# Last stage of an attention and two-MLP kernel: the out-projection as seven products of halves, and x read back as prepared parts

## The chip, the cores and the metric

The kernel runs on one core of a Trainium2 chip. A core has TensorE (PE in the profile; its weight loads are shown apart as PEld), VectorE (DVE), ScalarE (ACT), GpSimd (POOL) and SyncE (SP), whose queue issues all of this kernel's DMA transfers, in its program order. The metric is device time in microseconds (us); lower is better.

## The reference

Inputs are fp32. Block-causal attention is followed by two MLPs; each MLP's activations stand between its two matrices.

```python
def _moe_ref(x, w_in, w_out):      # x [2304, 512], w_in [512, 2048], w_out [2048, 512]
    h = x @ w_in
    g = h * np.cos(h)
    return (g @ w_out).astype(np.float32)
...
    r = np.maximum(h, 0.0)         # second MLP: same shapes, own weights
    g = r * r
    return (g @ w_out).astype(np.float32)
...
    attn_out = _attn_ref(**attn_kwargs)      # 4 batches, 8 heads, 576 rows, 64 wide
    x = np.ascontiguousarray(attn_out.transpose(0, 2, 1, 3)).reshape(B * S, H * D)
    x = _moe_ref(x=x, **moe_kwargs)
    return _moe2_ref(x=x, **moe2_kwargs)
```

## The kernel before

**Precision.** Every large product is taken in parts: an operand is split into a rounded part ("hi", an fp32r tile, made by `hi_part`) and the rest ("lo", by `lo_part`), and `mm3` issues three matmuls: hi*hi, hi*lo, lo*hi. A split costs one ScalarE and one VectorE instruction as a rule.

**Stages.** The 2048 wide middle of each MLP is cut in four column groups of 512. Attention runs first, together with the first half of MLP 1's middle (`first_in`, `first_out`, results kept in DRAM as `y1_d`). Then a loop over `stage` does the rest: stage 0 is the second half of MLP 1 and adds `y1_d`, giving `y_d`; stage 1 is the first half of MLP 2, kept in DRAM as `y2_d`; stage 2, the last, is the second half of MLP 2 and adds `y2_d`, giving `out`. Each stage goes over five chunks of tokens: four of 512 and one of 256 (called chunk 4).

**In-projection.** In these stages h is computed by seven products of halves instead of eight (`quad`, Winograd's form of Strassen's method): x and the weight block are each cut into 2 x 2 quarters, seven sums or differences of quarters ("forms") are split into hi and lo, and seven products of 256 x 256 by 256 tokens, 12 matmuls each, are accumulated in three PSUM banks `a`, `b`, `c`. `load_quarters` loads a chunk of x, makes the four sums and the seven splits, in every stage anew. Chunk 4 goes without (`two`, `load_plain`). The weights' forms are made once by `left_parts` ("staging") and kept in DRAM as `wi_d`; `factors` loads them.

**Out-projection.** In stages 1 and 2, for each 128 tokens, 24 matmuls with g as the stationary operand and 512 columns of `w2_out` as the moving one are accumulated in one PSUM bank `y`; VectorE adds `y2` in stage 2, and a DMA writes 128 tokens. The weights come as raw words of 8 bytes, are converted and split by `weights` (eight pieces per stage).

**Order.** Nothing is issued as the code is written: `Recorder` records operations and a list scheduler (`schedule`) puts them in order, with tables of numbers (`BIAS`, `PUT_OFF`, `LATE` and the like). The order on each engine is fixed when the program is built; an instruction that waits holds up all that stand behind it on its engine or queue.

Of the kernel before, what the change touches and what calls it, by code (L numbers as in the profile page):

```python
# [24 lines left out]
BIAS = [{"DVE": 1.89, "ACT": 0.46, "POOL": 0.26}, {"DVE": 2.58, "ACT": -0.56, "POOL": 0.68}, {"DVE": -0.3, "ACT": -2.99, "POOL": 0.29}, {"DVE": -1.17, "ACT": -3.72, "POOL": 2.36}]  # L25
# [14 lines left out]
PUT_OFF = [{"load": 114, "weights": -25, "prep": 11, "scores": 21, "weighted": -156, "split": 287, "in": 62, "cos": -140, "out": -54, "warm": 9160, "later": 877}, {"load": 381, "weights": -104, "prep": -71, "scores": 69, "weighted": -789, "split": 92, "in": 43, "cos": -127, "out": -24, "later": 911}, {"load": 543, "weights": 771, "prep": 52, "scores": 520, "weighted": 66, "split": 1698, "in": 0, "cos": -391, "out": -77, "later": 696}, {"in": 92, "out": 124, "later": -317}]  # L40
# [99 lines left out]
class Recorder:  # L140
# [9 lines left out]
    LATE, SLACK, EXTRA = 2497, 4, 16  # L150
# [204 lines left out]
def f(v):  # L355
    return v.bitcast(F32)
# [7 lines left out]
def kernel(  # L364
# [251 lines left out]
    y2_d = T(dram, [NT // 128, 128, DM], F32, "y2_d")  # L616
    wi_d = [[T(dram, [128, 2, 512], F32, f"wi_d{c}{i}") for i in range(7)] for c in range(6)]
# [134 lines left out]

    @of("weights")
    def left_parts(w, k, to):
# [3 lines left out]
        s1, s2, s3, s4 = [T(st_p, [128, 256], F32, f"ws{i}") for i in range(4)]  # L758
# [4 lines left out]
        cs = slice(k * 256, k * 256 + 256)  # L763
        for t, x in zip(to, (a11, a12, s4, a22, s1, s2, s3)):
            st = T(st_p, [128, 2, 256], F32R, "so", 2)
            hi_part(st[:, 0], x)
            lo_part(st[:, 1], x, st[:, 0])
            dma(t[:, :, cs], f(st), 262144)

    @of("later")  # L770
    def left_weights(w, c, to):

        gate = R.ops[-1:]
        for k in range(2):
            left_parts([weight_piece(w[i * 128:i * 128 + 128, c * 512:c * 512 + 512], gate) for i in (k, k + 2)], k, to)

# [66 lines left out]
    def in_cos(tmp, w_in, xs, g, n):  # L843

        for m in range(HALF):
# [8 lines left out]
            hi_part(g[0][:, m, :n], r)  # L854
            lo_part(g[1][:, m, :n], r, g[0][:, m, :n])

    @of("out")
    def out_T(w_out, g, n, sink):

        for d in range(KD):  # L860
            ps = bank("y")[:, :n]
            for m in range(HALF):
# [3 lines left out]
                    ps, (hi[m % 4][:, c], lo[m % 4][:, c]), (g[0][:, m, :n], g[1][:, m, :n]), m == 0, m == HALF - 1  # L866
# [256 lines left out]
    xs = {}  # L1123
# [12 lines left out]
    def new_g():  # L1136
        return [T(g_p, [128, HALF, 512], F32R, f"g{i}") for i in "hl"]
# [276 lines left out]
```

## Time and profile before

| What | Value |
|---|---|
| Median of 3 runs | 1003.09 us (1002.53 to 1003.45) |
| The profiled execution's own time | 1003.07 us |
| Span of the profiled execution, first to last instruction | 1001.3 us |
| TensorE busy | 978.8 us, 98% |
| VectorE, ScalarE, GpSimd busy | 663.3, 636.6, 203.6 us |
| DMA moved | 150.10 MB, mean 150 GB/s |
| Stage 2 | from about 805 us of the span to its end |

A matmul's duration in the trace includes its way through the array, and matmuls overlap, so the distance between the starts of two matmuls is what one costs; the busy share alone does not say that the engine does useful work all the time. "Idle before" and "waited for" are times in which an engine had nothing to do, with the instruction that ended it.

### The profile page before, as it was taken

What the parts mean: (1) busy time and instruction counts of PE and PEld (TensorE: products, weight loads), DVE (VectorE), ACT (ScalarE), POOL (GpSimd) and SP (SyncE); (2) the same over time, 40 slices, a digit from 0 to 9 for tenths busy, and PEclk for the clock granted to TensorE, in tenths of its full rate; (3) what the DMA queues carried; (4) which work ended last, traced back from release to release, by engine and by line L of the source; (5) the groups of instructions that cost most, each with busy time, mean ns of one, the idle gap of its engine ahead of it and who ended that gap; (6) DMA issues with size and microseconds to landing.
All of it is one profiled execution on the core that took longest, in us unless ns stands there. A gap on an engine that the chain in (4) does not pass through costs nothing.

```text
span 1001.3 us, 18384 instructions
## 1 busy us (share of the span) xinstructions
PE 978.8 (98%) x6672; PEld 862.2 (86%) x6672; DVE 663.3 (66%) x1469; ACT 636.6 (64%) x1423; POOL 203.6 (20%) x281
## 2 busy tenths in 40 slices
PE   7879999999999999999999999999999999999998
PEld 5647987889888989999898989898988898988987
DVE  4668565667676756485877977956859395835523
ACT  7898688898998996473675865654556471413301
POOL 4666143274554541000033100000000000000000
PEclk8979999999999999999999999999999999999999
DMA  7644233356555448822535698325366843222111
GB/s 191 183 132 124 59 90 88 101 137 182 172 171 170 149 146 298 310 68 85 172 102 167 206 305 312 126 85 189 119 219 210 323 161 98 68 67 64 43 64 43
DMA packets 136506, 150.10 MB, mean 150 GB/s; under 512 B 70368, under 2 KB 102624, under 8 KB 136416
## 3 DMA queue, kind: packets, MB, share of 16 engines
q1 hardware_dynamic: 136416, 148.93, 47.5%
q8 instruction: 53, 0.87, 0.4%
q14 instruction: 37, 0.30, 0.1%
HBM read 99.09 MB, written 49.81 MB: 149 GB/s over the span
## 4 chain that ended last, share of the span: by engine, by line
PE 89%; DVE 4%; ACT 3%; POOL 2%; issue 1%; DMA 1%; SPq 0%; POOLq 0%; DVEq 0%
PE y L530 40%; PE h L530 35%; PE t L547 6%; PE a L540 4%; PE s L540 3%; PE s L530 1%; DVE c L431 1%; DVE s L431 1%; DVE r L424 1%; POOL e L513 1%; ACT e L415 1%; POOL c L717 1%; DVE gl L472 0%; DMA raw<-in_moe_w_in_dram 0%; ACT c L415 0%
## 5 line engine op out<-in xcount | busy, mean ns | idle before, releaser
L530 PE MATMUL h<-xh,w 128*128 128x256 f32 x1536 | 289.1, 283 | 0.1
L530 PEld LDWEIGHTS h<-xh,w 128*128 128x128 f32 x1536 | 244.3, 191 | 2.6 <-ACT p L483 0.4
L530 PE MATMUL y<-gh,w 128*128 128x256 f32 (+2 forms) x832 | 211.8, 330 | 6.2 <-POOL w L449 3.2
L530 PE MATMUL h<-xl,w 128*128 128x256 f32 x768 | 216.6, 283 | 0.0
L530 PE MATMUL y<-w,gh 128*128 128x512 f32 x576 | 185.1, 395 | 0.0
L530 PEld LDWEIGHTS y<-gh,w 128*128 128x128 f32 x832 | 143.3, 189 | 20.0 <-issue 4.6
L530 PEld LDWEIGHTS h<-xl,w 128*128 128x128 f32 x768 | 146.9, 191 | 1.1
L530 PE MATMUL y<-gl,w 128*128 128x256 f32 (+2 forms) x416 | 135.6, 329 | 0.8 <-DVE gl L472 0.8
L530 PEld LDWEIGHTS y<-w,gh 128*128 128x128 f32 x576 | 107.6, 188 | 25.0 <-DVE w L472 0.2
L530 PE MATMUL y<-w,gl 128*128 128x512 f32 x288 | 113.8, 395 | 0.0
L454 ACT ACTIVATE gh<-r 128x512 fp32r<-128x512 f32 (+2 forms) x138 | 76.6, 556 | 50.5 <-DVE r L1292 34.0
L472 DVE TENSOR_TENSOR gl<-r,gh 128x512 fp32r<-128x512 f32 (+2 forms) x135 | 85.7, 639 | 27.6 <-ACT gh L454 24.9
L957 DVE CUSTOM_DVE_ANT_0 e<-s,mask 128x384 f32<-128x384 f32 (+4 forms) x160 | 71.0, 478 | 30.4 <-PE s L540 22.1
L513 POOL TENSOR_SCALAR e<-e,st 128x256 f32<-128x256 f32 (+4 forms) x124 | 75.3, 621 | 75.3 <-DVE st L978 55.6
L415 ACT ACTIVATE e<-e,st 128x128 f32<-128x128 f32 (+4 forms) x144 | 82.8, 578 | 4.9 <-DVE st L957 2.7
L530 PEld LDWEIGHTS y<-gl,w 128*128 128x128 f32 x416 | 78.2, 189 | 6.9 <-DVE gl L472 1.3
L424 DVE TENSOR_TENSOR o<-y,y 128x512 f32<-128x512 f32 (+1 forms) x38 | 25.2, 662 | 83.0 <-PE y L530 80.3
L483 ACT ACTIVATE p<-h 128x512 f32<-128x512 f32 x48 | 28.5, 593 | 74.7 <-PE h L530 74.7
L547 PE MATMUL t<-ident,e 128*128 128x128 f32 (+1 forms) x400 | 65.6, 288 | 2.2 <-POOL e L513 2.1
L530 PEld LDWEIGHTS y<-w,gl 128*128 128x128 f32 x288 | 54.1, 188 | 12.7
L483 ACT ACTIVATE r<-t 128x384 f32<-128x384 f32 (+1 forms) x110 | 56.1, 533 | 12.8 <-PE t L547 11.9
L530 PE MATMUL h<-xs2h,w 128*128 128x320 f32 x256 | 61.5, 313 | 0.0
(139 smaller groups left out, 1758.5 us busy)
## 6 DMA issues: line engine op xcount, KB each, us to landing
wi_d<-so SPq DMA_DIRECT2D x84, 256.0 KB, 3.0
w<-wi_d SPq DMA_DIRECT2D x42, 512.0 KB, 6.4
raw<-in_moe_w_in_dram SPq DMA_DIRECT2D x32, 512.0 KB, 5.1
raw<-in_moe_w_out_dram SPq DMA_DIRECT2D x32, 512.0 KB, 4.2
y<-y_d SPq DMA_DIRECT2D x34, 256.0 KB, 2.9
y_d<-o SPq DMA_DIRECT2D x34, 256.0 KB, 2.8
x<-y_d SPq DMA_DIRECT2D x16, 512.0 KB, 4.0
k<-in_k_dram SPq DMA_DIRECT2D x36, 128.0 KB, 2.8
```

The source lines that it names most:

```text
L415: return nc.scalar.activation(real(out), real(in_), func, **kw)
L424: out.size / 0.96 + 68, lambda: nc.vector.tensor_tensor(real(out), real(a), real(b), op=op), [out], [a, b],
L431: lambda: nc.vector.scalar_tensor_tensor(real(out), real(a), s, real(b), op0=op0, op1=op1),
L454: "ACT": ("ACT", n / 1.2 + 92, lambda: nc.scalar.activation(real(hi), real(x), ACTF.Copy)),
L472: lambda: nc.vector.tensor_tensor(real(lo), real(x), real(f(hi)), op=ALU.subtract), 1,
L483: "ACT": ("ACT", n / 1.2 + 50, lambda: nc.scalar.activation(real(out), real(ps), ACTF.Copy)),
L513: lambda: nc.gpsimd.tensor_scalar(real(out), real(x), real(s), 1.0, op0=ALU.mult, op1=ALU.mult),
L530: lambda: nc.tensor.matmul(real(ps), lhsT=real(lhsT), rhs=real(rhs), start=start, stop=stop, skip_group_check=True),
L540: nc.tensor.matmul(real(ps), lhsT=real(l), rhs=real(r), start=start, stop=stop, skip_group_check=True)
L547: lambda: nc.tensor.transpose(real(out), real(in_), real(ident)[0:rows, 0:rows]), [out], [in_, ident],
L717: lambda: nc.gpsimd.tensor_tensor(real(wi), real(t), real(wi), op=ALU.subtract), 1,
L957: lambda: nc.vector.tensor_tensor_reduce(out=real(e), in0=real(ps), in1=real(m), scale=-1.0, scalar=BIG, op0=ALU.add, op1=ALU.min, accum_o ...
```

## The change

Stage 2's out-projection is done by seven products as well. For each of the two column groups of 512, g (squared h) is cut into 2 x 2 quarters of 256 x 256 tokens; `formed` makes the seven forms of g out of `quad`'s four results with four sums, and splits each. `w2_out`'s forms are made by `right_parts_of` in stages 0 and 1, kept in DRAM as `wf_d`, and loaded by `right_factors` into tiles that stage 2 has no other use for. `out_quad` multiplies: per chunk seven products, each of 24 matmuls with 256 columns (12 in chunk 4, whose four quarters have 128 tokens). `second` adds the partial results in PSUM to `y2`, seven adds per chunk. The 14 splits and 8 sums per chunk replace 8 splits.

Stage 1 now writes each split form of x to DRAM (`xp_d`, 24 transfers of 512 KB) for the four chunks that it takes first; stage 2 loads these instead of `y_d`, with no sums and no splits. Stage 1 takes the chunks in the order 0, 4, 1, 2, 3, and stage 2 in the order 3, 0, 1, 2, 4, so that chunk 3's forms are still in place when stage 2 begins. Output and `y2` transfers are 256 tokens by 256 columns. `g` becomes eight small tiles, the output tile has four buffers instead of two, and the scheduler's tables are other ones, so the order changes in every stage.

```diff
-BIAS = [{"DVE": 1.89, "ACT": 0.46, "POOL": 0.26}, {"DVE": 2.58, "ACT": -0.56, "POOL": 0.68}, {"DVE": -0.3, "ACT": -2.99, "POOL": 0.29}, {"DVE": -1.17, "ACT": -3.72, "POOL": 2.36}]
+BIAS = [{"DVE": 1.72, "ACT": 0.3, "POOL": 0.23}, {"DVE": 3.65, "ACT": -0.74, "POOL": -0.23}, {"DVE": 0.06, "ACT": -1.78, "POOL": 0.06}, {"DVE": -1.43, "ACT": -5.31, "POOL": 1.15}]
...
-    LATE, SLACK, EXTRA = 2497, 4, 16
+    LATE, SLACK, EXTRA = 1369, 0, 27
...
+    def right_parts_of(w, k, to):
+        b11, b12, b21, b22 = [x[:, o:o + 256] for x in w for o in (0, 256)]
+        t1, t2, t3, t4 = four_sums()
+        add(t1, b12, b11, ALU.subtract)
+        add(t2, b22, t1, ALU.subtract)
+        add(t3, b22, b12, ALU.subtract)
+        add(t4, b21, t2, ALU.subtract)
+        stage_parts((b11, b21, b22, t4, t1, t2, t3), k, to)
...
+            if keep is not None:
+                dma(keep[j], f(t).rearrange("p j k c -> p (j k c)"), 524288)
...
+    def kept_parts(keep, which):
+        ops = {}
+        for j in which:
+            t = x_tile(j)
+            dma(f(t).rearrange("p j k c -> p (j k c)"), keep[j], 524288)
+            ops[j] = t[:, 0], t[:, 1]
+        return ops
...
+            if (i, j) == (0, 1):
+                add(a22, a21, a22)
+                add(a21, a11, a21, ALU.subtract)
+                add(a11, a22, a11, ALU.subtract)
+                split(4, a22)
+                split(5, a11)
+                split(6, a21)
+            if len(parts) == 4:
+                add(a12, a12, a11, ALU.subtract)
+                split(2, a12)
...
+        def times_(ps, i, first):
+            for t in range(nt):
+                cs = slice(t * 128, t * 128 + 128)
+                for q in range(2):
+                    (gh, gl), (wh, wl) = g[q][i], w[q][i]
+                    for m in range(2):
+                        mm3(
+                            ps[:, t], (gh[:, m, cs], gl[:, m, cs]), (wh[:, m], wl[:, m]),
+                            first and not t + q + m, q + m == 2, (a, b, c),
+                        )
+
+        times_(a, 0, True)
+        finish(0, 0, a, False)
+        times_(b, 1, True)
+        finish(0, 0, b, True)
+        times_(a, 5, False)
+        finish(0, 1, a, False)
+        times_(c, 4, True)
+        finish(1, 1, c, False)
+        times_(a, 6, False)
+        finish(1, 1, a, True)
+        times_(c, 2, False)
+        finish(0, 1, c, True)
+        times_(a, 3, False)
+        finish(1, 0, a, True)
...
+        def finish(h, d, ps, last):
+            t, r0 = ys[h, d], c0 + h * nt * 128
+            tt(t, ps, t, ALU.add)
+            if last:
+                dma(out[r0:r0 + nt * 128, d * 256:d * 256 + 256].rearrange("(t p) d -> p t d", p=128), t, nt * 131072)
...
+    ROUNDS = (0, 1, 2, 3, 4), (0, 4, 1, 2, 3), (3, 0, 1, 2, 4)
...
+                if turn_:
+                    xs = kept_parts(xp_d[i], FIRST if i < 4 else (0, 1, 4))
+                g = g_forms()
...
+            if (stage, turn_) in ((0, 3), (1, 0)):
+                right_weights(w2_out, 2 + stage, wf_d[stage])
```

**Where it moves instructions.** First place: VectorE at the very end of the program, chunk 4 of stage 2. In the names `h` is an in-projection's PSUM bank, `s` and `r` are squared h, `y` an out-projection's bank, `o` an output tile, and the tiles `gh`, `gl` followed by a number are, after the change, places of forms of g (each holds a form's hi and lo). Before, the last two in-projection banks (`h_12077`, `h_12107`) and the out-projection's adds:

```order
L424 TENSOR_TENSOR s_12111<-h_12077,s_12111 128x512
L472 TENSOR_TENSOR gl_12071<-s_12111,gh_12063 128x2x256
L424 TENSOR_TENSOR s_12140<-h_12107,s_12140 128x512
L472 TENSOR_TENSOR gl_12071<-s_12140,gh_12063 128x2x256
L424 TENSOR_TENSOR o_12169<-y_12137,y2_11997 128x512
L424 TENSOR_TENSOR o_12195<-y_12167,y2_12054 128x512
```

After the change, from the last in-projection bank (`h_12625`) to the form that the out-projection's fourth product needs:

```order
L424 TENSOR_TENSOR s_12694<-h_12625,s_12694 128x512
L424 TENSOR_TENSOR o_12473<-y_12666,o_12473 128x256
L472 TENSOR_TENSOR gh2_12706<-s_12694,gh2_12706 128x2x128
L472 TENSOR_TENSOR gl2_12708<-s_12694,gl2_12708 128x2x128
L733 TENSOR_TENSOR s_12694<-s_12670,s_12694 128x2x128
L733 TENSOR_TENSOR s_12670<-s_12670 128x2x128
L424 TENSOR_TENSOR o_12473<-y_12667,o_12473 128x256
L733 TENSOR_TENSOR s_12670<-s_12694,s_12670 128x2x128
L472 TENSOR_TENSOR gh3_12726<-s_12694,gh3_12726 128x2x128
L472 TENSOR_TENSOR gl1_12729<-s_12670,gl1_12729 128x2x128
L472 TENSOR_TENSOR gl0_12736<-s_12670,gl0_12736 128x2x128
L733 TENSOR_TENSOR s_12694<-s_12694,s_12670 128x2x128
```

Behind the last bank's square stood one lo part and two adds; now four sums, five lo parts and adds of partial results (`o_12473`) stand among each other. TensorE takes these forms in this order meanwhile (`raw_10203`, `so`, `x_10004`, `w` are forms of `w2_out`; 18 matmuls on forms of the first column group stand ahead):

```order
L530 MATMUL y_12666<-raw_10203,gh1_12689 128x256 x6
L530 MATMUL y_12666<-so_10607,c_12648 128x256
L530 MATMUL y_12666<-so_10625,c_12648 128x256
L530 MATMUL y_12666<-so_10607,n_12657 128x256
L530 MATMUL y_12666<-so_10607,c_12648 128x256
L530 MATMUL y_12666<-so_10625,c_12648 128x256
L530 MATMUL y_12667<-x_10004,gl2_12708 128x256 x2
L530 MATMUL y_12666<-so_10607,n_12657 128x256
L530 MATMUL y_12667<-x_10004,gl2_12708 128x256 x4
L530 MATMUL y_12668<-w_10644,gh3_12726 128x256 x4
```

A product that goes on in a bank (`y_12666`, from `gh1` to `so`) comes behind the VectorE add that reads this bank. Second place: VectorE in a full chunk of stage 2, after the change, from the sum that frees the bank of the chunk's last in-product to the lo part of the form that is ready last (`gl2_11411`):

```order
L424 TENSOR_TENSOR r_11348<-h_11238,p5_11329 128x512
L1358 SCALAR_TENSOR_TENSOR r_11336<-r_11336 128x512
L1358 SCALAR_TENSOR_TENSOR r_11348<-r_11348 128x512
L472 TENSOR_TENSOR gh0_11338<-s_11246,gh0_11338 128x512
L472 TENSOR_TENSOR gh1_11364<-r_11336,gh1_11364 128x512
L472 TENSOR_TENSOR gh2_11374<-r_11348,gh2_11374 128x512
L424 TENSOR_TENSOR s_11390<-h_11238,s_11390 128x512
L424 TENSOR_TENSOR r_11407<-h_11240,u2_11311 128x512
L1358 SCALAR_TENSOR_TENSOR r_11407<-r_11407 128x512
L472 TENSOR_TENSOR gl2_11411<-s_11390,gl2_11411 128x512
```

TensorE there has 24 matmuls of the first product behind its last in-product, and then these, the last of which is the first to need that lo part:

```order
L530 MATMUL y_11383<-x_9946,t2_11277 128x256 x2
L530 MATMUL y_11383<-x_9946,t3_11309 128x256
L530 MATMUL y_11383<-x_9946,t2_11277 128x256 x2
L530 MATMUL y_11383<-x_9946,t3_11309 128x256
L530 MATMUL y_11383<-x_10004,gl2_11411 128x256 x2
L530 MATMUL y_11384<-w_10633,c_11263 128x256 x2
L530 MATMUL y_11384<-w_10633,c_11280 128x256
L530 MATMUL y_11384<-w_10633,c_11263 128x256
L530 MATMUL y_11383<-x_10004,gl2_11411 128x256 x4
```

Before, the VectorE rows at that point of a chunk held the splits of the next chunk's x among the squares and lo parts of g:

```order
L472 TENSOR_TENSOR xl4_11110<-t0_10811,xh4_11091 128x512
L1292 SCALAR_TENSOR_TENSOR r_11103<-r_11103 128x512
L424 TENSOR_TENSOR r_11125<-h_10954,u2_11059 128x512
L472 TENSOR_TENSOR xl2_11134<-x_10785,xh2_11116 128x512
L1292 SCALAR_TENSOR_TENSOR r_11125<-r_11125 128x512
L424 TENSOR_TENSOR s_11136<-h_10952,s_11136 128x512
L472 TENSOR_TENSOR gl_10946<-r_11103,gh_10937 128x2x256
```

Third place: SP's queue where stage 0 passes into stage 1. `y_d` is stage 0's result, `x` the raw tile that stage 1 loads, `raw` a piece of weights. Before, after chunk 4's last write of `y_d` came three loads of weights (`w`), two raw pieces and chunk 1's loads:

```order
L553 DMA y_d_6512<-o_8445 128x256
L553 DMA w_8493<-wi_d36_8008 128x1024
L553 DMA w_8501<-wi_d32_7809 128x1024
L553 DMA w_8509<-wi_d33_7881 128x1024
L695 DMA raw_8616<-in_moe2_w_out_dram 128x4096
L695 DMA raw_8624<-in_moe2_w_out_dram 128x4096
L553 DMA x_8681<-y_d_6512 128x2x512
```

After the change chunk 4 is loaded at once, and writes of kept parts (`xp_d`) and of `w2_out`'s forms (`wf_d`) stand between the loads:

```order
L553 DMA y_d_6716<-o_8452 128x256
L553 DMA xp_d40_8631<-x0_8589 128x1024
L553 DMA wf_d06_8650<-so_8634 256x1x256
L553 DMA wf_d00_8325<-so_8639 256x1x256
L553 DMA x_8671<-y_d_6716 128x2x256
L697 DMA raw_8697<-in_moe2_w_out_dram 128x4096
L553 DMA wf_d01_8333<-so_8706 256x1x256
L553 DMA wf_d02_8459<-so_8717 256x1x256
L697 DMA raw_8768<-in_moe2_w_out_dram 128x4096
```

TensorE has 77 matmuls of 256 columns and 18 of 512 between the last matmul of stage 0 (whose bank goes into `o_8452`) and the first that needs `x_8671`'s parts.

## Rows read from the trace of the kernel before

**Rows 1.** The page: busy time by engine, and two lines of its 40 slices.

```profile
PE 978.8 (98%) x6672; PEld 862.2 (86%) x6672; DVE 663.3 (66%) x1469; ACT 636.6 (64%) x1423; POOL 203.6 (20%) x281
PEclk8979999999999999999999999999999999999999
```

**Rows 2.** What PE waited for from 100 us on, the two longest: total, times, longest.

```profile
PE y L530 <- DVE gl L472: 0.8, 2, 0.4
PE t L547 <- POOL e L513: 0.3, 1, 0.3
```

**Rows 3.** What PE waited for in the first 100 us, the two longest.

```profile
PE y L530 <- POOL w L449: 3.2, 2, 2.9
PE y L530 <- issue: 2.6, 1, 2.6
```

**Rows 4.** Windows: busy time by engine (x instructions), clock, DMA share, GB/s; last one is stage 2.

```profile
550.00:600.00 50.00, 49.65 (x322) 45.15 (x321) 44.46 (x80) 35.32 (x65) 3.49 (x4) 1.00 0.79 254
805.00:998.00 193.00, 192.56 (x1199) 172.77 (x1198) 102.55 (x163) 61.35 (x108) 0.00 (x0) 1.00 0.22 70
```

**Rows 5.** PE's timeline in stage 2: start, duration, operation; in-projection, then out-projection.

```profile
866.49 0.40 PE L530 MATMUL h<-xh,w 128*128 128x256 f32 x2
...
866.85 0.40 PE L530 MATMUL h<-xh,w 128*128 128x256 f32 x2
...
867.32 0.63 PE L530 MATMUL y<-w,gh 128*128 128x512 f32 x2
...
868.03 0.63 PE L530 MATMUL y<-w,gh 128*128 128x512 f32 x2
```

**Rows 6.** Groups by line: weight loads, and VectorE at 256 columns.

```profile
L530 PEld LDWEIGHTS y<-gh,w 128*128 128x128 f32 x832 | 143.3, 189 | 20.0 <-issue 4.6 <-POOL w L449 4.1 <-DVE w L472 0.8
L424 DVE TENSOR_TENSOR o<-y,y 128x256 f32<-128x256 f32 x4 | 1.7, 421 | 1.5 <-PE y L530 1.5
```

**Rows 7.** VectorE's timeline in stage 2: dependent, then independent instructions behind each other.

```profile
892.77 0.69 DVE L424 TENSOR_TENSOR r<-h,p 128x512 f32<-128x512 f32 x1 [1.29 <-PE h L530]
893.50 0.69 DVE L1292 SCALAR_TENSOR_TENSOR r<-r 128x512 f32<-128x512 f32 x1
...
903.21 0.69 DVE L472 TENSOR_TENSOR gl<-s,gh 128x512 fp32r<-128x512 f32 x1
903.81 0.69 DVE L424 TENSOR_TENSOR r<-h,p 128x512 f32<-128x512 f32 x1
```

**Rows 8.** Timeline of the last 15 us, ScalarE, VectorE and TensorE's last matmul.

```profile
986.45 0.60 ACT L415 ACTIVATE s<-h 128x512 f32<-128x512 f32 x1 [0.89 <-PE h L530]
987.08 0.69 DVE L424 TENSOR_TENSOR s<-h,s 128x512 f32<-128x512 f32 x1 [0.79 <-ACT s L415]
987.81 0.63 ACT L454 ACTIVATE gh<-s 128x512 fp32r<-128x512 f32 x1 [0.76 <-DVE s L424]
988.47 0.69 DVE L472 TENSOR_TENSOR gl<-s,gh 128x512 fp32r<-128x512 f32 x1 [0.70 <-ACT gh L454]
997.16 0.40 PE L530 MATMUL y<-w,gl 128*128 128x512 f32 x1
997.60 0.69 DVE L424 TENSOR_TENSOR o<-y,y 128x512 f32<-128x512 f32 x1 [4.91 <-PE y L530]
```

**Rows 9.** The chain that ended last, its last stretch: start, us, what.

```profile
986.35 11.22 PE y L530 x48
```

**Rows 10.** DMA from 570 to 610 us: share of 16 engines; issues, KB, us to landing.

```profile
q1 hardware_dynamic: 6252, 12.32, 91.5%
x<-y_d SPq DMA_DIRECT2D x2, 512.0 KB, 8.5
y_d<-o SPq DMA_DIRECT2D x4, 256.0 KB, 3.5
```

**Rows 11.** DMA issues of the whole run: KB each, median us to landing.

```profile
y_d<-o SPq DMA_DIRECT2D x20, 128.0 KB, 2.0
x<-y_d SPq DMA_DIRECT2D x4, 256.0 KB, 2.8
```

More of the change, by code (lines that the diff above doesn't have):

```diff
@@ L751, in w_tile, with stage_parts, four_sums @@
         return T(pool, [128, 2, 512], F32R, "w", n)
+    def stage_parts(forms, k, to):
+        cs = slice(k * 256, k * 256 + 256)
+        for t, x in zip(to, forms):
+            st = T(st_p, [128, 2, 256], F32R, "so", 2)
+            hi_part(st[:, 0], x)
+            lo_part(st[:, 1], x, st[:, 0])
+            dma(t[:, :, cs], f(st), 262144)
+    def four_sums():
+        return [t[:, i] for t in [T(st_p, [128, 2, 256], F32, f"ws{i}") for i in range(2)] for i in range(2)]
     @of("weights")
@@ L853, in in_cos @@
             tt(r, h, r, ALU.mult)
-            hi_part(g[0][:, m, :n], r)
-            lo_part(g[1][:, m, :n], r, g[0][:, m, :n])
+            hi, lo = [row(x, m)[:, :n] for x in g]
+            hi_part(hi, r)
+            lo_part(lo, r, hi)
     @of("out")
@@ L1136, in new_g, with row @@
     def new_g():
-        return [T(g_p, [128, HALF, 512], F32R, f"g{i}") for i in "hl"]
+        return [[T(g_p, [128, 2, 512], F32R, f"g{i}{m}") for m in range(HALF // 2)] for i in "hl"]
+    def row(g, m):
+        return g[m // 2][:, m % 2]
     def first_in(b, r):
@@ L1251, in two @@
             for j in range(2):
-                product(ps, w, left[j], xs[j * (i + 1)], not j)
+                product(ps, w, left[j], xs[(0, 1, 4)[j * (i + 1)]], not j)
             sink(i, 0, ps)
@@ new lines, in formed, with split, take @@
+    @of("cos")
+    def formed(g, parts, n):
+        def split(i, x):
+            hi, lo = [t[:, :, :n] for t in g[i]]
+            hi_part(hi, x)
+            lo_part(lo, x, hi)
+        def take(i, j, r):
+            parts[i, j] = r
+            if (i, j) != (0, 1):
+                split({(0, 0): 0, (1, 1): 3, (1, 0): 1}[i, j], r)
+            if len(parts) < 4 and (i, j) != (0, 1):
+                return
+            a11, a12, a21, a22 = [parts.get(x) for x in ((0, 0), (1, 0), (0, 1), (1, 1))]
+            if (i, j) == (0, 1):
[8 more added lines that the diff above has]
+                split(2, a12)
+        return take
@@ new lines, in out_quad, with y_bank @@
+    @of("out")
+    def out_quad(g, w, nt, n, finish):
+        def y_bank():
+            return bank("y").rearrange("p (t d) -> p t d", t=2)[:, :nt]
+        a, b, c = y_bank(), y_bank(), y_bank()
+        def times_(ps, i, first):
[3 more added lines that the diff above has]
+                    (gh, gl), (wh, wl) = g[q][i], w[q][i]
+                    for m in range(2):
+                        mm3(
[16 more added lines that the diff above has]
+        finish(1, 0, a, True)
```

157 lines of the change are left out of this document (108 added, 49 removed).

## The prediction

> **What bounds the kernel now.** I read the page first. TensorE is busy 98% of the span, at full granted clock but for the opening slices, while VectorE and ScalarE are busy two thirds of it [rows 1]. A busy TensorE can still wait, so the waits come next: from 100 us on the two longest sums are 0.8 and 0.3 us [rows 2], and in the window of stage 2 it is busy 192.56 of 193 us [rows 4]. So a matmul taken out of the late stages is worth its full distance to the next, as long as the other engines and DMA keep up. The opening 100 us are different: TensorE waits there for weights being converted [rows 3], and the scheduler's new order may move that either way.
>
> The distance between starts is the price of a matmul. In stage 2 three 256-column ones take 866.49 to 866.85, 0.120 us each [rows 5]; the last 48 of 512 columns take 11.22 us, 0.234 each [rows 9], which the rows of the timeline repeat within a hundredth.
>
> **The change part by part.** The sum is made against the profiled execution: 1003.07 us, a span of 1001.3 and 1.8 around it. It lies at the median (1003.09).
>
> 1. *Matmuls.* Per full chunk 4 x 24 matmuls of 512 columns go (96 x 0.234 = 22.5 us), and 7 x 24 of 256 come (168 x 0.120 = 20.2): 2.3 us less, 9.2 for four chunks. Chunk 4 is taken in point 3. Each new matmul has its own weight load, as each in-projection matmul has now, and those run at 0.120 with their loads hidden, so I take 0.120.
>
> The Trainium skill speaks against this: "TensorE: Matmul & The Clock Gate", section "Back-to-back issue gap", says that in streams of weight loads and matmuls the spacing is about 81 ns at 128 columns and 131 at 512. An estimate halfway by columns between them, some 98 ns, would make 756 matmuls 17.5 us dearer than the 432 they replace. The trace disagrees at both ends of this kernel: 120 ns at 256 columns and 234 at 512 [rows 5, 9].
>
> 2. *Does VectorE keep up in the four full chunks?* VectorE now has, per chunk, 6 sums of banks with copies, 8 squares, 8 new sums of forms, 14 lo parts and 7 adds to `y2`, 43 instructions; TensorE has 40.3 us (336 matmuls). At 0.60 us, the distance of independent instructions, that is 26 us, at 0.73, that of dependent ones, 31 [rows 7]. On the average there is room; the question is the hand-over. Count from the moment at which the last in-product gives way to the out-projection. The order (second place) lets VectorE begin with `r_11348` when product 6 ends, 24 matmuls earlier, plus 0.2 us, the lag from a matmul's slot to VectorE (997.60 against 997.16 + 0.234) [rows 8]: at -2.7. Ten instructions, one of them dependent on its neighbour, put the start of the lo part of `gl2` at +2.9 and its end at +3.6. Its hi part is earlier: ScalarE reads the bank at +0.1, the square starts at +0.73, hi at +1.46, lo could start at +2.12, as the same chain does now, with the slot at 986.35 [rows 8, 9]. TensorE wants it behind 24 + 8 + 4 matmuls, at +4.3. So there is 0.7 us of slack and no stall. Were every distance 0.73 instead, it would come 0.4 us late, four times: 1.8 us at most. I take 0, since most neighbours in that order do not depend on each other.
>
> What stage 2 no longer does (four chunks' x splits and sums, eight weight pieces) was hidden: TensorE waits for none of it now [rows 4]. It is worth nothing by itself, but it is what makes room for the new sums. The reads of kept parts are 7 x 512 KB per chunk in 40 us, in a stage whose DMA share is 0.22 [rows 4]; each part is free one chunk's products ahead, at least 18 us before it is wanted. Taken as 0, and it would cost only if a read took over twice the 8.5 us that a 512 KB load took in the fullest stretch [rows 10]. `w2_out`'s forms likewise stand in the queue behind the last stage-1 products with some 24 us until the first of them in stage-1 places is used.
>
> 3. *Chunk 4, the end.* Here nothing follows to fill TensorE, and the order (first place) mixes adds that wait for banks with the lo parts that the next products need. Zero is again 986.35. Instructions of 256 columns last 0.42 us [rows 6] and follow each other in some 0.34, 0.60 less half a row's worth. TensorE does 18 matmuls of the first column group and 6 with `gh1`: +2.9. The add of `y_12666` starts at +3.1, ends at +3.5, and only then may product 5 go on in that bank: 0.7 us lost. `gl2` is ready then; product 1 ends at +5.0. The second add of `o_12473` waits for it (+5.2 to +5.6), and behind this add stand a sum and the lo part of `gh3`, ready at +6.3, where TensorE wants it at +5.1 plus one matmul: 1.1 us lost. One more bank costs 0.2. With 84 matmuls (10.1 us) and 2.0 us lost, TensorE is done at +12.05, and the last add ends at +12.7. Before, it ended at 998.29 [rows 8], +11.9. Cost 0.7; if the reordering lost nothing, it would be a gain of 1.3, if each hand-over took twice as long, a cost of about 2.7. The last transfer stays as it is but for its size (128 instead of 256 KB); nothing taken.
>
> 4. *From stage 0 to stage 1.* Chunk 4 now comes second, right after its `y_d` is written. The chain: last matmul, add (0.2 + 0.42), write, read, hi and lo (0.63 + 0.69), and two issues in the queue, taken as 0.5 us each from neighbouring issues. With 2.0 and 2.8 us for the transfers [rows 11] it takes 7.7, with the 3.5 and 8.5 of the stretch of before in which DMA was 91.5% busy [rows 10] 14.9. What covers it: 77 x 0.120 + 18 x 0.234 = 13.5 us of matmuls (third place). So between 0 and 1.5 us are lost, and more if the queue holds the read up; I take 1.5, since the new writes (2.1 MB of kept parts, 3.5 MB of forms) come into this very stretch.
>
> 5. *Staging `w2_out`* twice (per time, 8 sums and 14 splits of 256 columns more than whole pieces had) adds some 15 us of VectorE per time. In the fullest 50 us VectorE has 5.5 us free, ScalarE 14.7, GpSimd 46.5 [rows 4]; the scheduler gives this work low urgency. Hidden, 0; what it could cost is in the first rival. The attention's new order is taken as 0, between the bounds of the third.
>
> Sum: -9.2 + 0.7 + 1.5 = -7.0: **996.1 us.**
>
> **The rivals.** *First, slower: SP's queue at stage 0 to 1.* A write of a kept part waits in the queue until VectorE has its lo part, and the raw pieces of stage 1's `w2_out`, which the interleaved out-projection needs, stand behind it (third place). Ten such writes (three of chunk 4, seven of chunk 0 or 1) that each hold the queue for one split, 0.63 + 0.69 us and hand-overs, 1.4 in all, would make TensorE 14 us late: 1003.1 - 8.5 + 14 = 1008.6. For it: DMA is 91.5% busy there already [rows 10] and VectorE 89% [rows 4]. Against it: stage 1's matmuls can go ahead without these weights for a chunk. It decides at 8.5 us, 0.85 per write.
>
> *Second, slower: weight loads set the pace.* If a load of 189 ns [rows 6] bound each of the 756 matmuls, they would take 143 instead of 101 us: 1003.1 + 42 = 1045. It decides at 0.134 us per matmul. The in-projection, same stationary and moving sizes, runs at 0.120 [rows 5], so I give it little.
>
> *Third, faster: the opening.* The new order begins the first out-projection with more other matmuls ahead of its weights. If the 3.2 us for GpSimd's weights [rows 3] go and the join of point 4 costs nothing: 996.1 - 4.7 = 991.4. By the same rows it could as well add as much (999.3).
>
> *Fourth, no change:* the join and the end each cost double and more, and half of the first rival comes: about 1002.
>
> **How the numbers follow.** The forecast with its own spread (993 to 999.5) has a chance of 0.61, the third rival's faster side 0.12, its slower side and VectorE's 1.8 us 0.07, the fourth 0.08, the first 0.10, the second 0.02. The range, 991.5 to 1002.5, leaves out most of the first two slow rivals and the edge of the third. This kernel's measurement tells 0.2% (2 us) from no change: under 1001.1 is faster, 0.80; within, 0.08; slower, 0.12.
>
> **What would show it.** After: about 756 matmuls of 256 columns on `y` in stage 2 at 0.120 us; no wait of TensorE within chunks 0 to 3 of stage 2; some 2 us of waits for `gl`, `gh` or `o` on VectorE in the last 13 us; a wait for `x1` or for stage 1's `w` at the join of under 2 us. A spacing over 0.13, waits of TensorE over 5 us at the join, or an opening that differs by over 4 us would make the number wrong.

## The result and the profile after

The changed kernel takes **992.92 us** (median of 4 runs, 992.57 to 995.70) where the kernel before takes 1002.81 (4 runs, 1002.29 to 1003.45): a ratio of **0.9907, 95% interval 0.9888 to 0.9926**. It is faster, by 9.9 us where 7.0 were forecast. The profiled execution takes 993.0 us, with a span of 991.2. In a later set of runs the same kernel took 991.37 against 1003.54.

The page after, which answers to [rows 1]: 324 more matmuls (756 in, 432 out), and TensorE still busy 98% of a shorter span.

```profile
PE 969.4 (98%) x6996; PEld 869.7 (88%) x6996; DVE 661.1 (67%) x1486; ACT 646.7 (65%) x1450; POOL 246.9 (25%) x339
```

What TensorE waited for from 100 us on (in total, times, longest); [rows 2] had a longest sum of 0.8 us. Of these five, the second and the third lie in chunk 4's out-projection at the end, the other three ahead of stage 2.

```profile
PE y L530 <- ACT gh L454: 1.0, 1, 1.0
PE y L530 <- DVE gh L472: 0.9, 1, 0.9
PE y L530 <- DVE o L424: 0.5, 1, 0.5
PE h L530 <- ACT p L483: 0.4, 1, 0.4
PE y L530 <- POOL gl L468: 0.4, 1, 0.4
```

The same view of the first 100 us, beside [rows 3]: the wait for GpSimd's weights grew from 3.2 to 5.5 us, the 2.6 us of "issue" are gone.

```profile
PE y L530 <- POOL w L449: 5.5, 2, 3.3
```

The windows, in the columns of [rows 4] (the second is stage 2). The fullest stretch has DMA at 0.92 of its time instead of 0.79; stage 2 has it at 0.45 instead of 0.22, and VectorE at 122 of 185 us.

```profile
550.00:600.00 50.00, 49.02 (x266) 41.72 (x266) 40.45 (x74) 32.85 (x62) 1.49 (x2) 1.00 0.92 315
805.00:990.00 185.00, 181.43 (x1524) 180.62 (x1522) 122.06 (x205) 60.62 (x107) 0.00 (x0) 1.00 0.45 158
```

**Where the time went.** Stage 2's first in-product starts at 804.70 us before and at 804.74 after, so in these two executions nothing is gained or lost ahead of it. From there to the end of the span it is 196.6 us before and 186.5 after: stage 2 holds all of the 10.1 us. TensorE's timeline shows why, in the form of [rows 5] (start, duration, operation, count):

```profile
824.87 0.87 PE L530 MATMUL y<-raw,ws 128*128 128x256 f32 x6
825.58 0.88 PE L530 MATMUL y<-raw,gh 128*128 128x256 f32 x6
...
846.50 1.72 PE L530 MATMUL h<-x,w 128*128 128x256 f32 x13
```

Six of the new matmuls take 0.71 us from group to group, 0.118 each; the thirteen in-projection matmuls of the same size take (1.72 - 0.28) / 12 = 0.120. From one chunk's in-products to the next it is 39.87 us (846.50 to 886.37), where it was 42.51 (848.08 to 890.59): 2.64 less per chunk.

The end of chunk 4, TensorE first, beside [rows 8, 9]. The out-projection's first matmul starts at 986.19 before:

```profile
986.19 0.63 PE L530 MATMUL y<-w,gh 128*128 128x512 f32 x2
```

(The 986.35 of [rows 9] is a link of the chain, 0.16 us later; after the change that view has 975.86.) After, it starts at 975.69, and both are counted from these starts here.

```profile
975.69 0.87 PE L530 MATMUL y<-raw,ws 128*128 128x256 f32 x6
...
977.81 0.87 PE L530 MATMUL y<-raw,gh 128*128 128x256 f32 x6
979.20 0.50 PE L530 MATMUL y<-so,c 128*128 128x256 f32 x2 [0.52 <-DVE o L424]
...
980.71 0.45 PE L530 MATMUL y<-w,gh 128*128 128x256 f32 x2
982.06 0.50 PE L530 MATMUL y<-w,gh 128*128 128x256 f32 x2 [0.90 <-DVE gh L472]
...
982.86 0.62 PE L530 MATMUL y<-w,gl 128*128 128x256 f32 x4
983.54 0.73 PE L530 MATMUL y<-w,gh 128*128 128x256 f32 x4
...
987.06 0.84 PE L530 MATMUL y<-w,gh 128*128 128x256 f32 x6
```

And VectorE there: the add for which the bank waits, the split that stands behind another add, and the last add.

```profile
978.72 0.42 DVE L424 TENSOR_TENSOR o<-y,o 128x256 f32<-128x256 f32 x1 [0.18 <-PE y L530]
...
980.91 0.42 DVE L424 TENSOR_TENSOR o<-y,o 128x256 f32<-128x256 f32 x1 [0.30 <-PE y L530]
981.25 0.41 DVE L733 TENSOR_TENSOR s<-s 128x256 f32<-128x256 f32 x1
981.58 0.42 DVE L472 TENSOR_TENSOR gh<-s,gh 128x256 fp32r<-128x256 f32 x1
...
987.94 0.42 DVE L424 TENSOR_TENSOR o<-y,o 128x256 f32<-128x256 f32 x1 [0.93 <-PE y L530]
```

(`gh` stands here for the place in which the lo part lies.) The add that has to free the bank starts at +3.03. From 977.81 to 979.20 TensorE takes 1.39 us for six matmuls that take 0.71 elsewhere: 0.68 lost. The bracket shows only 0.52 idle, since it counts from the end of a matmul, and a matmul of 256 columns lasts 0.28 in the trace where the next can start after 0.12. The second add, a sum and then the split run from +5.2 to +6.3, and 1.35 us pass where two matmuls take 0.24: 1.11 lost, with 0.90 in the bracket. One more bank costs 0.21 (982.86 to 983.54 for four matmuls) and no bracket shows it. The last add ends at 988.36, +12.67. Before it ended at 998.29, +12.10.

### The profile page after: what moved, and what is told of

It is laid out like the page before. It is cut to its first block, busy times and chain, and to the rows that moved or that the text cites. A ratio compares the mean times of both kernels' runs of the same rounds, so it can differ in the third digit from the quotient of the medians.

```text
span 991.2 us, 19381 instructions
## 1 busy us (share of the span) xinstructions
PE 969.4 (98%) x6996; PEld 869.7 (88%) x6996; DVE 661.1 (67%) x1486; ACT 646.7 (65%) x1450; POOL 246.9 (25%) x339
## 4 chain that ended last, share of the span: by engine, by line
PE 85%; DMA 6%; ACT 4%; DVE 3%; issue 1%; POOL 1%; SPq 0%; ACTq 0%
PE y L530 37%; PE h L530 32%; PE t L547 6%; PE a L540 5%; PE s L540 3%; DMA wi_d<-so 3%; PE s L530 1%; DMA x<-x_d 1%; DMA raw<-in_moe_w_in_dram 1%; DVE c L431 1%; ACT e L415 1%; DMA w<-wi_d 1%; ACT c L415 0%; ACT r L415 0%; ACT t L415 0%
## 5 line engine op out<-in xcount | busy, mean ns | idle before, releaser
L530 PE MATMUL h<-x,w 128*128 128x256 f32 x2304 | 301.2, 283 | 0.6 <-ACT p L483 0.4
L530 PEld LDWEIGHTS h<-x,w 128*128 128x128 f32 x2304 | 291.2, 191 | 4.2 <-ACT p L483 1.4
L530 PE MATMUL y<-w,gh 128*128 128x512 f32 (+1 forms) x450 | 118.9, 354 | 1.0 <-DVE gh L472 0.9
L513 POOL TENSOR_SCALAR e<-e,st 128x128 f32<-128x128 f32 (+4 forms) x133 | 79.3, 611 | 59.8 <-DVE st L1026 32.4
L530 PE MATMUL y<-w,gl 128*128 128x256 f32 (+1 forms) x306 | 80.5, 334 | 0.0
L424 DVE TENSOR_TENSOR o<-y,o 128x512 f32<-128x512 f32 (+1 forms) x55 | 35.0, 636 | 53.9 <-PE y L530 49.9
L431 DVE SCALAR_TENSOR_TENSOR c<-raw,c 128x512 int32<-128x512 int32 x64 | 50.5, 789 | 17.8 <-POOL c L719 17.3
L547 PEld LDWEIGHTS t<-ident,e 128*128 128x128 f32 (+1 forms) x400 | 46.8, 143 | 15.2 <-POOL e L513 7.2
L483 ACT ACTIVATE p<-h 128x512 f32<-128x512 f32 x48 | 28.4, 592 | 48.2 <-PE h L530 48.1
L415 ACT ACTIVATE t<-raw,minus 128x512 int32<-128x512 int8 x64 | 48.8, 762 | 16.2 <-DMA raw<-in_moe_w_in_dram 7.6
L468 POOL TENSOR_TENSOR gl<-r,gh 128x256 fp32r<-128x256 f32 (+1 forms) x53 | 44.4, 843 | 51.0 <-ACT gh L454 47.1
```

Of the source, the lines that this page charges most:

```text
L415: return nc.scalar.activation(real(out), real(in_), func, **kw)
L424: out.size / 0.96 + 68, lambda: nc.vector.tensor_tensor(real(out), real(a), real(b), op=op), [out], [a, b],
L431: lambda: nc.vector.scalar_tensor_tensor(real(out), real(a), s, real(b), op0=op0, op1=op1),
L468: lambda: nc.gpsimd.tensor_tensor(real(lo), real(x), real(f(hi)), op=ALU.subtract), 1,
L483: "ACT": ("ACT", n / 1.2 + 50, lambda: nc.scalar.activation(real(out), real(ps), ACTF.Copy)),
L513: lambda: nc.gpsimd.tensor_scalar(real(out), real(x), real(s), 1.0, op0=ALU.mult, op1=ALU.mult),
```

## The experiments

Each kernel is timed in alternation with the kernel before on its chip, and the ratio is to that one (1003.05 us in the first set, 1003.54 in the second, 1003.17 in the third). The theory: seven products save matmul time in stage 2, and the rest of the change is cover for it. The rivals: the kept parts alone, or the scheduler's new numbers alone, bring the gain.

**The kept parts without the seven products.** Stage 2's out-projection is that of before, so `w2_out`'s forms are neither staged nor read; the kept parts, the order of the chunks and the scheduler's numbers are those of the changed kernel.

```diff
-            w2f = right_factors()
...
-            if (stage, turn_) in ((0, 3), (1, 0)):
-                right_weights(w2_out, 2 + stage, wf_d[stage])
...
-            if stage == 2:
-                second(i, c0, g, w2f)
-                continue
...
+                    w2o = weights(wa_p, row_chunks(w2_out, 2 * stage - 2, 2 * stage))
```

> The changed kernel with stage 2's out-projection as before (24 matmuls of 512 columns per 128 tokens, weights converted in stage 2, no forms of w2_out staged), but with x's kept parts, chunk order and tables of after. Theory: the kept parts save nothing by themselves, so 1001 to 1005 us and a chunk of stage 2 every 42.5 us, as before. Rival (kept parts are worth something alone): 1000 us or less, with a chunk in under 42 us.

Measured: **999.26 us, ratio 0.9959 (0.9944 to 0.9974)**. Faster than expected. Stage 2's chunks follow each other at 42.48 us as they did (42.51). TensorE begins its first unbroken row of stage 2's in-projection matmuls at 802.45, and from there to the end of the span it is 195.4 us, 1.2 less than before. But ten of the stage's 768 in-projection matmuls have run by then, one by one among the last matmuls of stage 1:

```profile
799.05 0.28 PE L530 MATMUL h<-x,w 128*128 128x256 f32 x1
...
802.11 0.28 PE L530 MATMUL h<-x,w 128*128 128x256 f32 x1
...
802.45 3.76 PE L530 MATMUL h<-x,w 128*128 128x256 f32 x30
```

Ten times 0.120 is the 1.2 us. For the same work stage 2 takes 196.6 us, as before: the kept parts with their order bring nothing in it, as the theory says. From this kernel to the changed one, the seven products alone shorten stage 2 by 196.6 - 186.5 = **10.1 us**. What makes this kernel faster than the one before lies ahead of stage 2, in the profile 1.7 us in the opening (first in-product of stage 0 at 415.5 instead of 417.2) and 1.7 between that in-product and stage 2 (385.8 instead of 387.5, the ten matmuls left out). So the expectation that nothing else pays was wrong by some 2 us; which of the order, the numbers and the kept parts brings them was not tried.

**The splitting work put back in stage 2.** The kept parts are read, and ScalarE and VectorE do over each of them, in place, a copy and a maximum as large as the splits were.

```diff
-            ops[j] = t[:, 0], t[:, 1]
+            hi, lo = t[:, 0], t[:, 1]
+            act(hi, f(hi), ACTF.Copy)
+            tt(lo, f(lo), f(lo), ALU.max)
+            ops[j] = hi, lo
```

> The changed kernel with work put on each kept part that stage 2 loads: ScalarE copies its hi part in place, VectorE takes the maximum of its lo part with itself, which leaves the values as they are and costs about what the splits cost. VectorE then has 50 instead of 43 instructions per full chunk. Theory (VectorE has room on average and some 0.7 us of slack at the hand-over): 993 to 995.5 us, waits of TensorE within chunks under 0.6 us each. Rival (the kept parts are what makes the seven products pay): 997 us or more, TensorE waiting 1 us and more in each chunk.

Measured: **993.68 us, 0.9903 (0.9888 to 0.9918)**. The window of stage 2, in the columns above:

```profile
805.00:990.00 185.00, 180.35 (x1513) 179.14 (x1511) 136.45 (x229) 72.61 (x130) 0.00 (x0) 1.00 0.44 155
```

VectorE has 14.4 us more there and ScalarE 12.0, and stage 2 lasts 187.7 us (from 803.46) instead of 186.5; one new wait of TensorE for `gh` on ScalarE (0.9 us) is most of the 1.2. So TensorE's neighbours have room for the new sums even with the old work. That the kept parts are what makes the products pay falls.

**The scheduler's numbers of before.** The changed kernel with `BIAS`, `PUT_OFF` and the three constants of before.

```diff
-    LATE, SLACK, EXTRA = 1369, 0, 27
+    LATE, SLACK, EXTRA = 2497, 4, 16
```

> The changed kernel with the scheduler's tables of before (BIAS, PUT_OFF, LATE, SLACK, EXTRA). Theory (the whole gain is the smaller spacing sum of TensorE's matmuls in stage 2, some 10 us, and the order is only its carrier): 991 to 997 us, stage 2 still some 186 us long, differences only as waits in the opening or at the joins. Rival (the new tables are a good part of the gain): 998 us or more.

Measured: **1027.28 us, 1.0240 (1.0222 to 1.0258)**, 34 us slower than the changed kernel. My theory, that the order merely carries the change, falls: stage 2 starts 26.0 us later than in the changed kernel's first profile (830.74), and it lasts 195.5 us, not 186. Of its waits from 640 to 800 us (stage 1), the longest sum:

```profile
PE y L530 <- ACT w L454: 9.2, 6, 3.6
```

What ScalarE did there, in its timeline (the bracket is how long it sat idle and what released it):

```profile
673.06 0.42 ACT L454 ACTIVATE so<-c 128x256 fp32r<-128x256 f32 x1 [1.58 <-DMA wf_d<-so]
673.38 0.75 ACT L415 ACTIVATE c<-raw,minus 128x512 int32<-128x512 int8 x1
...
675.61 0.63 ACT L454 ACTIVATE w<-c 128x512 fp32r<-128x512 f32 x1 [1.18 <-DVE c L431]
```

A split `so` of a new form sits until the write of a form ahead has freed its buffer (1.58 us here, 2.03 at 666.23). Directly behind it on ScalarE stands the first step of converting a raw piece (`c<-raw`), and the weights `w` of the out-projection that TensorE is about to run wait for that piece. In the queue, 12 waits for `so` on VectorE take 23.4 us between 600 and 700 us. This is near the first rival, since staging holds up stage 1's own weights, but by way of the splits' buffers, and not of raw pieces that stand behind writes in the queue. The waits are not the whole price. In the windows around them (TensorE's busy time comes first behind the length; the clock is the third number from the end) the granted clock is lower:

```profile
600.00:700.00 100.00, 84.64 (x549) 75.53 (x549) 70.37 (x127) 53.34 (x99) 0.00 (x0) 0.93 0.81 289
800.00:860.00 60.00, 54.19 (x334) 49.12 (x334) 31.77 (x60) 21.90 (x44) 0.00 (x0) 0.91 0.76 265
```

The shortfalls, 0.07 of 100 us and 0.09 of 60, are up to 12 of the 34 us.

**The same numbers, one group at a time.** First the three constants alone, then `PUT_OFF` alone.

> The changed kernel with the scheduler's three waiting constants of before (2497, 4 and 16 for 1369, 0 and 27), its other numbers kept. All numbers of before together cost 34 us. If the assumed lateness of DMA is what matters (2.5 us instead of 1.4 makes it order work with loads earlier or later), most of it is seen here: 1010 and over, with waits for w in stage 1. If the urgencies matter, this stays within 991 to 998.

> The changed kernel with the urgencies by kind of work of before, its other numbers kept. If they are what the 34 us hang on (prep 52 instead of 752 in stage 1 puts the preparing of w2_out's forms ahead of the out-projection's own weights), most of it is seen here: 1010 and over, with waits of TensorE for w between 650 and 800 us. If not, 991 to 998.

Measured: **1018.09 us, 1.0144 (1.0130 to 1.0158)** with the constants, **1022.93, 1.0199 (1.0185 to 1.0213)** with `PUT_OFF`. Either one brings back the greater part of the loss, and the longest waits in stage 1 are of the same kind; from 640 to 800 us, with the constants:

```profile
PE y L530 <- ACT w L454: 4.8, 3, 3.3
```

and with `PUT_OFF`:

```profile
PE y L530 <- ACT w L454: 7.2, 5, 2.3
```

The two losses, 25 and 30 us, are each near the 34 us of all three groups and do not add up to them, so no single group carries the loss. They lie in different places: with the constants stage 2 lasts 195.0 us and starts 14.3 us late (818.99), with `PUT_OFF` it lasts 186.5, as in the changed kernel, and starts 28.4 us late (833.14). `BIAS` was not tried by itself.

**The new numbers in the kernel before.** The lines of the last diff the other way, `BIAS` and `PUT_OFF` too, and no other change.

> The kernel before with the scheduler's numbers of the changed one, and no other change. Theory (each set of numbers fits its own program): slower than before by some us, 1005 to 1015, with waits of TensorE for weights or forms. Rival (the new numbers are better for any program, and part of the gain is theirs): faster, 998 to 1001, with the gain in the opening or at the joins and nothing changed in stage 2.

Measured: **1009.63 us, 1.0061 (1.0047 to 1.0075)**, slower by 6.1 us, with waits of TensorE for `gh` of 5.4 us between 415 and 640 us. The new numbers are no gain in themselves; each set fits its own program.

**The forms staged later.** Both stagings of `w2_out`'s forms behind the first two chunks of stage 1. What it aims at is the longest new wait of the changed kernel, in ScalarE's timeline there:

```profile
583.56 0.42 ACT L454 ACTIVATE so<-ws 128x256 fp32r<-128x256 f32 x1 [1.26 <-DMA wi_d<-so]
583.89 0.58 ACT L483 ACTIVATE r<-h 128x512 f32<-128x512 f32 x1
584.36 0.62 ACT L454 ACTIVATE gh<-r 128x512 fp32r<-128x512 f32 x1
```

A split waits 1.26 us for its buffer, whose write is late (from 580 to 590 us the DMA queue's share is 105.8%), and `gh` stands two behind it; TensorE waits 0.98 us for it until 585.04.

```diff
-            if (stage, turn_) in ((0, 3), (1, 0)):
-                right_weights(w2_out, 2 + stage, wf_d[stage])
+            if stage == 1 and turn_ < 2:
+                right_weights(w2_out, 2 + turn_, wf_d[turn_])
```

> The two stagings of w2_out's forms come behind the first and second chunk of stage 1, instead of behind the fourth chunk of stage 0 and the first of stage 1. Theory: in the changed kernel TensorE waits 1.0 us for gh at 584 us because ScalarE waited 1.26 us for a so buffer whose write was late while all DMA engines were busy (share 1.03 to 1.06 from 570 to 590 us); with a staging less there the wait goes, and the time is 990 to 991.5. Rival: the DMA and the order of the preparing work in stage 1 have no room for it either; waits of over 1 us for w, x or gl come between 600 and 800 us, and the time is 993 to 1000. Second rival: the wait at 584 us stays as it is, since DMA is as full there without these writes (it was 1.03 with the old out-projection as well), and the time is that of the changed kernel, 991.5 to 993.

Measured: **1013.80 us, 1.0104 (1.0090 to 1.0118)**. Its windows, in the same columns:

```profile
810.00:820.00 10.00, 3.02 (x17) 2.31 (x16) 8.70 (x18) 4.98 (x10) 0.00 (x0) 0.82 0.52 178
820.00:830.00 10.00, 5.03 (x23) 5.04 (x24) 1.70 (x4) 2.96 (x7) 0.00 (x0) 0.50 0.79 249
830.00:840.00 10.00, 5.11 (x25) 4.52 (x24) 5.84 (x9) 2.17 (x5) 0.00 (x0) 0.67 0.97 320
```

The theory's place is right: the wait at 584 us is gone, TensorE does not wait from 560 to 800 us, and stage 2 starts at 801.08. The kernel without the seven products, which stages no forms, has no wait there either, with DMA as full (1.04 from 580 to 590 us), so a full DMA alone does not make it. But the price comes where neither rival put it, at the opening of stage 2, which lasts 210.9 us; TensorE's longest waits from 805 to 850 us:

```profile
PE h L530 <- DMA w<-wi_d: 7.2, 1, 7.2
PE y L530 <- ACT gh L454: 4.1, 1, 4.1
PE y L530 <- ACT t L454: 2.8, 1, 2.8
PE y L530 <- DVE t L472: 2.0, 1, 2.0
```

With two short ones they make 17.8 of the 24.4 us by which stage 2 is longer; the windows above, at 0.50 to 0.82 of the clock, hold the rest.

What SP's queue waited for, from 780 to 850 us:

```profile
SPq L553 <- DVE so L472: 23.8, 16, 8.0
```

Stage 2's own in-weights are staged in stage 1 as well, now with the second staging of forms among them. Between 811.0 and 819.9 us the queue holds five writes `wi_d<-so` that wait for VectorE's lo parts, and the read `w<-wi_d` that TensorE wants is issued behind them, at 820.63. The forms `t` of the first chunk stand behind splits of the same staging on ScalarE, one of which sat 2.37 us for its buffer until 810.09. In the changed kernel the same view has 9.3 us in 6 waits.

**The short chunk fourth in stage 2.** So that a full chunk is last and its matmuls cover the hand-overs.

```diff
-    ROUNDS = (0, 1, 2, 3, 4), (0, 4, 1, 2, 3), (3, 0, 1, 2, 4)
+    ROUNDS = (0, 1, 2, 3, 4), (0, 4, 1, 2, 3), (3, 0, 1, 4, 2)
```

> Stage 2 takes its chunks in the order 3, 0, 1, 4, 2, so that a full chunk is the last. Theory (chunk 4's 1.4 us of waits are there because nothing follows it): 991.3 to 992.6 us, no wait in chunk 4, and the last full chunk ends with under 0.7 us of waits. Rival (any last chunk waits for VectorE, a full one with its 512-column instructions longer): 993 to 995 us.

Measured: **988.91 us, 0.9862 (0.9847 to 0.9877)**. Both waits at the end are gone; TensorE waits for nothing after 790 us, and stage 2 lasts 986.8 - 801.66 = 185.1 us where the changed kernel has 186.5 and, in its second profile, 186.4. So 1.3 us are its own, seen in the profile; the rest of the difference lies ahead of stage 2, where both run the same program. The same move with the forms staged later:

> The same, and the short chunk fourth in stage 2. Theory: the two gains add up (1.4 us at the end, 1 us at 584 us): 987.5 to 989.5, the fastest of all. Rival: as above for the forms; then it is 991 or more, and the kernel with the fourth place alone stays the fastest.

Measured: **1012.91 us, 1.0094 (1.0080 to 1.0108)**, with the waits of the later staging (7.7 us for `w<-wi_d`), and again nothing lost at the end.

**The short chunk third in stage 1, alone and with the move above, beside the changed kernel once more.**

```diff
-    ROUNDS = (0, 1, 2, 3, 4), (0, 4, 1, 2, 3), (3, 0, 1, 2, 4)
+    ROUNDS = (0, 1, 2, 3, 4), (0, 1, 4, 2, 3), (3, 0, 1, 2, 4)
```

> The changed kernel once more, on one chip with the three that follow, so that they have it beside them. Theory: 993 us (992 to 995), as its four runs. What it also tells is how far the opening wanders: its first in-product of stage 0 stood at 416.5 us, its granted clock in the first 100 us was 0.90. If the opening is a property of the order, both come back within 0.5 us; if it wanders with the execution, by up to 2 us.

> Stage 1 takes its short chunk third instead of second, so that its rows of y_d are read one chunk later; nothing else. Theory: the join cost about 0.7 us (the waits for gh of 1.0 and for p of 0.4 near it), so at most 1 us is to be had: 992 to 993.5. Rival: the order of chunks is worth what the tables are worth, since the scheduler's numbers were made for the old order; then this comes out slower, as the kernel with the tables of before did, by 5 us or more: 998 and over.

> The short chunk third in stage 1 and fourth in stage 2. Theory: the gain of the fourth place in stage 2 (1.4 us of waits at the end, by the profile 1.3 us of stage 2) and what the third place in stage 1 gives are in different places and add up: 990 to 992 if the short chunk's third place gives 0 to 1, and 988 to 989 if all of the 4 us seen with the fourth place alone is real. Rival: the two moves upset the order of the preparing work at the join, and waits for w of several us appear between 640 and 800 us: over 995.

Measured: the changed kernel **991.37 us, 0.9877 (0.9864 to 0.9891)**; third in stage 1 **994.68, 0.9905 (0.9892 to 0.9919)**; both moves **991.84, 0.9883 (0.9870 to 0.9897)**. Reading `y_d` a chunk later brings nothing: the join's waits are not for x at all. (The wait for `p` of 0.4 us that the expectation counts near the join lies at 774.59.) They are for `gh`: 0.7 us in the changed kernel's second profile, 2.0 with the third place alone and 1.2 with both moves, which are the same program up to there. Four profiles that run the changed kernel's program at this place (two of it, and those of the splitting work and of the fourth place) have 0.5 to 1.6 us at the longest of these waits, so the difference cannot be put down to the edit. The last section shows what followed the longest of them. Within stage 2 the fourth place is again worth some 1.5 us (990.6 - 805.72 = 184.9, against 186.4).

The changed kernel's second profile begins stage 0 at 415.3 us (416.5 in the first) and stage 2 at 802.66 (804.74): the same instructions wander by 2 us there, so a difference of that size ahead of stage 2 is put down to nothing. For the same reason the fourth place is shown to be faster in stage 2, but as a whole its interval, up to 0.9877, touches that of the changed kernel in the second set.

## Why the prediction was right, and where it was off

The forecast was 996.1 us, the range 991.5 to 1002.5. The result, 992.92, lies near the fast edge, and 991.37, of the later set, just outside. The mechanism was right: the matmuls of stage 2 cost less, and nothing in its full chunks waits for the new sums. The matmuls and the join were mis-sized to the pessimistic side, the staging was not free, and at the end two misses cancel.

1. **Matmuls, -9.2: mis-sized.** From the start of stage 2 to the first matmul of chunk 4's out-projection it is 181.49 us before (to 986.19) and 170.95 after (to 975.69), -10.5. Nearly all of the 1.3 us of difference comes from the step "those run at 0.120 with their loads hidden, so I take 0.120": at 0.118 for 168 matmuls a chunk comes out 0.34 us lower, and the chunks did, 2.64 instead of 2.3, four times. With the ends, stage 2 is shorter by 10.1 us, all of it by the products, as the kernel without them shows (-9.2 + 0.7 = -8.5 was forecast).

The rule that was weighed against the trace, "TensorE: Matmul & The Clock Gate" of the Trainium skill, section "Back-to-back issue gap", gave some 98 ns by the estimate and a loss of 17.5 us. The trace does not agree: the new matmuls are 118 ns apart and those that they replace 234.

2. **VectorE keeps up, 0: right.** TensorE waits for nothing between 780 and 975 us. The room was larger than the 0.7 us worked out for one hand-over suggested: 14.4 us more of VectorE's work in stage 2 cost 1.2 us. The sentence that the dropped splits are "what makes room for the new sums" was therefore wrong. (The bound beside it, 0.4 us four times, is 1.6 and not 1.8; nothing hangs on it.) The reads of the kept parts landed after 8.6 us (median from 805 to 840 us, at 0.91 of DMA's time), and nothing waited for them.

3. **Chunk 4's end, +0.7: right in size, in part by luck.** It was +0.57 to the last add (+12.67 against +12.10) and +0.4 to the span's end. The forecast counted the new kernel from the first matmul's start and the old one from 986.35, the link of the chain, which made the old end 0.16 us too short; counted alike, its own sum gives +0.6. TensorE's part came out at +12.05, as forecast, but as 9.7 us of matmuls and 2.3 lost, where 10.1 and 2.0 stood. The stalls are at the named instructions and have the named sizes (0.68 for 0.7, 1.11 for 1.1, 0.21 for 0.2); the first matmul behind each takes 0.1 us more than the others, which nobody had counted, and the matmuls came closer together (down to 0.113 us), which makes up for it.

4. **Stage 0 to stage 1, +1.5: mis-sized, and with another cause.** Ahead of stage 2 the sum of all differences was 0.0 us in one profile and -2.0 in the other; without the opening it is +0.8 and -0.2. The step that failed is "between 0 and 1.5 us are lost... I take 1.5": the cover of 13.5 us sufficed for the chain through `y_d`, at the transfers' time of that stretch. What TensorE waits for is `gh`, behind a split that waits for its buffer: 1.0 us, and 0.5 to 1.6 in the four profiles that run this program there.

5. **Staging, 0: mis-sized, and cheap for this order only.** From stage 0's first in-product to stage 2's it is 385.8 us in the kernel that stages no forms, and 386.8 to 389.3 in four profiles of kernels that are the changed one up to stage 2. So some 1 to 3.5 us go with it where it stands, the waits of point 4 among them; there is one profile without it, and the stretch wanders. The margin is thin: with the numbers of before the time grows by 34 us, and by 21 with the forms staged one and two chunks later. **The first rival** did not come in this order: TensorE waits for no `w` of stage 1. In other orders staging did hold these weights up, by way of the splits' buffers, and with the lower clock and the opening of stage 2 the price was above the rival's 14 us. **The second** (weight loads) is excluded by the spacing. **The third** (the opening) came to -0.7 us in one profile and -1.9 in the other, within its wandering.

## What to carry to other kernels

Where TensorE is busy 98% of the time, count the matmuls of a stage, take the distance between starts from the same stage, and the sum comes near (here -9.2 for -10.5); walk the last chunk instruction by instruction, since nothing covers its hand-overs, and put a full chunk last (1.3 to 1.5 us here). Take a loss from the distance between starts: a bracket of idle time leaves part of it out. Work that is "hidden" because it has a low urgency is hidden only in one order: ask which buffers it shares with urgent work and what stands behind its writes in the queue, for there the price was 21 to 34 us. Numbers that set a schedule belong to one program; carry the program over, and make them anew.

## What the runs showed of the hardware

**A wait can cost twice, and its length alone does not tell when.** With the short chunk third in stage 1, TensorE waits 1.78 us and then runs at half its clock for some 3.4 us. The windows of 1 us (TensorE's busy time, then the clock):

```profile
585.00:586.00 1.00, 0.89 (x4) 1.00 1.04 391
586.00:587.00 1.00, 1.00 (x4) 0.52 1.07 408
587.00:588.00 1.00, 1.00 (x4) 0.50 1.06 424
588.00:589.00 1.00, 1.00 (x4) 0.50 0.98 399
589.00:590.00 1.00, 1.00 (x5) 0.78 1.05 398
```

Its timeline over the same stretch:

```profile
585.11 0.50 PE L530 MATMUL y<-gh,w 128*128 128x512 f32 x1 [1.78 <-ACT gh L454]
...
587.57 1.05 PE L530 MATMUL y<-gh,w 128*128 128x512 f32 x2
588.42 0.63 PE L530 MATMUL y<-gl,w 128*128 128x512 f32 x1
```

Two matmuls of 512 columns take 0.85 us from start to start of what follows, 0.425 each instead of 0.234: the lower level, 1.2 GHz, granted about one microsecond after the wait ended. It costs another 1.7 us (the clock's shortfalls in these windows, 0.48 + 0.50 + 0.50 + 0.22; at half a clock each, 3.4 us). In the changed kernel the wait at the same place is 0.98 us, and the clock stays at 1.00 there; in the kernel with both moves, the same program up to here, it is 0.99 us, and in the one with the splitting work put back, there the same program as the changed kernel, 1.60 us, and the clock stays too. The kernel before with the new numbers has two waits of one length:

```profile
480.58 0.72 PE L530 MATMUL y<-gh,w 128*128 128x512 f32 x2 [1.76 <-ACT gh L454]
525.14 0.96 PE L530 MATMUL y<-gh,w 128*128 128x512 f32 x3 [1.76 <-ACT gh L454]
```

Behind the first the clock is 1.00 from 480 to 486 us; behind the second it is 0.67 from 526 to 528 us and 0.50 from 528 to 530. What decides between them is open. Nor does this explain the spread of the five times of the third-place kernel: the mean granted clock is 0.990 in its slowest, 996.02, and 0.989 in its fastest, 992.12. Where TensorE waited 7.2 us, as the forms staged later made it, the ten microseconds from 820 us show 0.50.

**Spacing at one size differs.** Matmuls of 256 columns stand 0.118 us apart in the out-projection and 0.120 in the in-projection, and at the end 0.113 (six from 986.38 to 987.06). Why is open; no run here varied it.
